# An unused tile of 224 bytes at the top of the right side of SBUF

## The chip, the cores and the metric

One Trainium2 chip, one of its cores. The metric is the time of one execution on the device in microseconds (us), the median of several runs. A single execution is also recorded by the hardware profiler, and every number about single instructions below is from that record. SBUF has 128 partitions; an address here is a number of bytes within a partition.

## The reference, cut to what matters

Attention with two mixes over the heads ("talking heads"), then two feed-forward blocks, all in float32:

```python
# q, k, v: (2, 12, 448, 64)
scores = einsum('bhij,hg->bgij', q @ k.T / 8, w_pre)
attn   = softmax(scores, axis=-1)
x      = einsum('bhij,hg->bgij', attn, w_post) @ v     # -> (896, 768)
h = x @ moe_w_in                                       # (768, 2048)
x = where(h > 0, h, exp(min(h, 0)) - 1) @ moe_w_out    # (2048, 768)
h = x @ moe2_w_in
out = (h * sigmoid(h)) @ moe2_w_out                    # (896, 768)
```

## The kernel before, in words

The order of all work is written out by hand; nothing is moved by a scheduler. The program has two parts.

**Attention** (functions `qk_pair`, `premix`, `postmix`, `av_pair`). In steps of 20 query rows TensorE computes the scores `pq` of a pair of heads (L107, K tiles `kt` stream through, Q tiles `qt` are the weights), VectorE and ScalarE write them to the tile `s`, a DMA on SP's queue (`relayout`, L137) lays them out as `blk`, and TensorE mixes the heads (`pre`, L149), then, after the softmax, mixes again (`post`, L188) and multiplies with V (`av`, L214). These matmuls are in float32 and use a quarter of the array each, four side by side.

**Two feed-forward blocks** (`moe_in`, `moe_out1`, `moe_in`, `moe_out2`). Here each product is split into high and low parts of type float32r, and three of the four part products are added up, so one chunk of weights gives three matmuls for each 128 rows of the contraction. All of these use the whole array and load new weights (128 columns) for each matmul:

- `ph` (L488): weights are the converted chunk `we`, the activations `x` stream through, 448 columns. 1152 matmuls: 576 in each block.
- `po` (L541): weights `we`, the gated activations `g` (`ge` for the first three) stream through, 448 columns. 576 matmuls.
- `py` (L561 to L563): weights `g` (`gf`), the chunk `we` streams through, 384 columns. 672 matmuls.

The weight chunks come from HBM as 64-bit numbers (`wr`), ScalarE and VectorE turn them into float32 (`wc`) and into the high and low parts (`we`) while TensorE works on earlier chunks.

**Where the tiles lie.** SBUF is shared out from both ends. Pools opened with `side="left"` grow upwards; pools with `side="right"` grow downwards from the end of the tile space, byte 229,344, which is 895 x 256 + 224. On the right lie:

- pool `qkt`: `kt` (later `x0`, the half of `x` for the first batch), `qt` (later three buffers of `we`);
- pool `s0`: `s` (later `x1`, the other half of `x`), pool `s1`: `s` and the tile `wz` of the warm-up matmuls;
- pool `wst`, which takes the place of `s1` in the last steps of attention: `wr`, `wc` and the fourth buffer of `we`.

The sizes of all of these (3584, 6144, 21,504 and 3072 bytes) are multiples of 256, so each starts 224 bytes past a multiple of 256. The parts of `x` and `we` that a matmul reads begin at multiples of 512 bytes from the start of the tile (128 columns of `we`), of 1536 (384 columns of `we`) or of 1792 (448 columns of `x`), all multiples of 256, so they too begin 224 bytes past one. On the left, `g`, `ge`, `gf`, `blk` and V begin 128 bytes past a multiple of 256, and so do the parts of `g` that `po` and `py` read; `pe` (the softmax's output), `krn` and `a` begin 64 past one.

```python
cm_w, wp = pool("qkt", bufs=1, side="right")
cm_s0, sp0 = pool("s0", bufs=1, side="right")
cm_s1, sp1 = pool("s1", bufs=1, side="right")
# moe_in, L488: stationary we, moving x
nc.tensor.matmul(ph, wt[:, kk * P:(kk + 1) * P], xq[hf, kk][:, xi], ...)
# moe_out1, L541: stationary we, moving g
nc.tensor.matmul(po, wt[:, kk * P:(kk + 1) * P], g_out1(k0 + kk, gi, hf), ...)
# moe_out2, L561: stationary g, moving we
nc.tensor.matmul(py, gh, hi[:, w_], start=(kf == 0), stop=False)
```

Of the kernel before, what the change touches and what calls it, by code (L numbers as in the profile page):

```python
# [7 lines left out]
F32 = mybir.dt.float32  # L8
# [9 lines left out]
P = 128  # L18
# [19 lines left out]
def attn_moe_moe(ctx: ExitStack, tc: tile.TileContext, q, k, v, w_pre, w_post, w1i, w1o, w2i, w2o, out):  # L38
# [4 lines left out]
    def pool(name, **kw):  # L43
        cm = tc.tile_pool(name=name, reuse_waits="tile", **kw)
        return cm, cm.__enter__()

    cm_c, cp = pool("const", bufs=1, side="left")
    cm_w, wp = pool("qkt", bufs=1, side="right")
    cm_s0, sp0 = pool("s0", bufs=1, side="right")
    cm_s1, sp1 = pool("s1", bufs=1, side="right")  # L50
# [635 lines left out]
            moe_out2(n, a, b_)  # L686
    cm_m.__exit__(None, None, None)

    for cm in (cm_pm, cm_g, cm_c, cm_ws, cm_s0, cm_w):
        cm.__exit__(None, None, None)  # L690


# [54 lines left out]
```

## Time and profile before

| | |
|---|---|
| median of 3 runs | 657.47 us (656.14 to 660.39) |
| the profiled execution | 654.97 us |
| its span, first to last instruction | 653.2 us |
| granted TensorE clock, mean | 0.997 of 2.4 GHz |
| TensorE busy | 643.3 us, 98% |
| VectorE, ScalarE, GpSimd busy | 375.3, 331.3, 55.3 us |

In the profile PE is TensorE's matmuls and PEld its weight loads, which overlap them; DVE is VectorE, ACT ScalarE, POOL GpSimd, SP SyncE, and an engine's name with a q its queue. L488 is line 488 of the kernel. The duration of one matmul is longer than the distance to the next, since matmuls follow each other in a pipeline: what sets the time is the distance from start to start, called the pitch below. A float32 matmul of the attention appears as two records. The row `post` of L488 is `ph` as well, written to a PSUM bank that the attention had.

### The profile page before, as it was taken

To read this page: it belongs to the slowest core of one execution; us is meant where nothing else is said; L and a number is where in the kernel's file an instruction comes from. 1 tells how busy PE (TensorE), PEld (TensorE's weight loads), DVE (VectorE), ACT (ScalarE), POOL (GpSimd) and SP (SyncE) were. 2 spreads that over 40 slices of the span, in tenths; PEclk is the share of its full clock that TensorE was granted. 3 is DMA by queue.
4 is the path that set the end of the run, shared out by engine and by line. 5 is a ranking of instruction groups with operands and counts; after the bars stand their busy time and mean duration, and the time that the engine had idled before them with its cause. 6 is when DMAs were issued, how large, how long until landed. Compare 5 with 4: busy or idle time off the path is not lost.

```text
span 653.2 us, 15579 instructions
## 1 busy us (share of the span) xinstructions
PE 643.3 (98%) x6444; PEld 557.6 (85%) x6444; DVE 375.3 (57%) x767; ACT 331.3 (51%) x693; POOL 55.3 (8%) x109
## 2 busy tenths in 40 slices
PE   7989999999999999999999999999999999999997
PEld 2556666677789999999999999999999999999997
DVE  3767777887637666666443345467676775307201
ACT  3656677788647767675223233455555554205101
POOL 2222222236300000000000000000000000000000
PEclk9989999999999999999999999999999999999999
DMA  5667537763304433335323444233443355317002
GB/s 177 227 185 234 174 107 206 236 214 122 125 3 135 121 108 97 103 108 151 95 83 99 129 129 146 72 98 98 120 120 98 96 149 191 96 57 224 22 1 85
DMA packets 37243, 82.36 MB, mean 126 GB/s; under 512 B 4100, under 2 KB 18228, under 8 KB 37172
## 3 DMA queue, kind: packets, MB, share of 16 engines
q1 hardware_dynamic: 36452, 80.61, 40.6%
q8 instruction: 51, 0.84, 0.5%
q10 hardware_dynamic: 720, 0.75, 0.3%
q14 instruction: 20, 0.16, 0.1%
HBM read 59.24 MB, written 2.75 MB: 95 GB/s over the span
## 4 chain that ended last, share of the span: by engine, by line
PE 98%; DMA 0%; issue 0%; ACT 0%; DVE 0%; ACTq 0%
PE ph L488 35%; PE po L541 18%; PE pre L149 8%; PE av L214 7%; PE post L188 6%; PE py L561 6%; PE py L562 6%; PE py L563 6%; PE pq L107 5%; PE post L488 1%; PE warm L250 1%; DMA blk<-s 0%; ACT L237 0%; ACT pe L163 0%; DVE nmx L155 0%
## 5 line engine op out<-in xcount | busy, mean ns | idle before, releaser
L488 PE MATMUL ph<-x,we 128*128 128x448 f32 x1116 | 228.1, 366 | 0.0
L488 PEld LDWEIGHTS ph<-x,we 128*128 128x128 f32 x1116 | 209.1, 188 | 19.4 <-issue 3.0
L541 PE MATMUL po<-g,we 128*128 128x448 f32 x468 | 99.5, 362 | 0.0
L541 PEld LDWEIGHTS po<-g,we 128*128 128x128 f32 x468 | 87.8, 188 | 5.8
L393 ACT ACTIVATE wr<-wr 128x384 f32<-128x384 f32 x132 | 70.7, 547 | 32.2 <-DMA wr<-in_w1o_dram 17.8
L436 DVE TENSOR_TENSOR we<-wc,we 128x768 fp32r<-128x768 f32 (+1 forms) x63 | 58.7, 932 | 45.2 <-ACT we L427 42.3
L163 ACT ACTIVATE pe<-pre,nmx 124x448 f32<-124x448 f32 (+1 forms) x92 | 57.4, 628 | 43.0 <-DVE nmx L155 42.5
L415 DVE SCALAR_TENSOR_TENSOR wc<-wr,wc 128x384 int32<-128x384 int32 x132 | 72.0, 545 | 5.5
L427 ACT CAST we<-wc 128x768 fp32r<-128x768 f32 (+1 forms) x63 | 50.8, 807 | 42.2 <-PE py L563 30.7
L188 PEld LDWEIGHTS post<-krn,pe 60*64 60x64 f32 x2520 | 49.8, 136 | 20.4 <-issue 15.0
L561 PE MATMUL py<-we,g 128*128 128x384 f32 x182 | 61.7, 339 | 0.0
L563 PE MATMUL py<-we,g 128*128 128x384 f32 x182 | 61.6, 339 | 0.0
L562 PE MATMUL py<-we,g 128*128 128x384 f32 x182 | 61.6, 338 | 0.0
L155 DVE TENSOR_REDUCE nmx<-pre 124x1 f32<-124x448 f32 (+1 forms) x92 | 53.1, 619 | 14.5 <-PE pre L149 13.7
L149 PE MATMUL pre<-blk,kpre 64*64 64x448 f32 (+1 forms) x360 | 53.6, 568 | 2.0 <-DMA blk<-s 1.2
L188 PE MATMUL post<-krn,pe 60*64 60x60 f32 x2520 | 50.5, 220 | 2.1 <-issue 2.1
L176 POOL TENSOR_SCALAR krn<-kps,sum 124x60 f32<-124x60 f32 (+1 forms) x92 | 40.9, 459 | 126.4 <-DVE sum L172 95.7
L107 PE MATMUL pq<-kt,qt 64*64 64x448 f32 (+2 forms) x384 | 50.2, 547 | 0.0
L413 DVE TENSOR_SCALAR wc<-wr 128x384 int32<-128x384 int32 x132 | 45.9, 348 | 0.0
L214 PE MATMUL av<-a,v 128*64 128x120 f32 (+1 forms) x768 | 45.6, 265 | 0.0
L503 ACT ACTIVATE e<-ph 128x448 f32<-128x448 f32 x32 | 17.4, 545 | 50.6 <-PE ph L488 50.6
L214 PEld LDWEIGHTS av<-a,v 128*64 128x64 f32 x768 | 36.9, 136 | 2.8 <-issue 0.3
(59 smaller groups left out, 624.8 us busy)
## 6 DMA issues: line engine op xcount, KB each, us to landing
blk<-s SPq DMA_DIRECT2D x90, 210.0 KB
wr<-in_w1i_dram SPq DMA_DIRECT2D x32, 384.0 KB
wr<-in_w2i_dram SPq DMA_DIRECT2D x32, 384.0 KB
wr<-in_w2o_dram SPq DMA_DIRECT2D x32, 384.0 KB
wr<-in_w1o_dram SPq DMA_DIRECT2D x24, 384.0 KB
v<-in_v_dram SPq DMA_DIRECT2D x16, 192.0 KB
wr<-in_w1o_dram SPq DMA_DIRECT2D x12, 256.0 KB
qt<-in_q_dram SPq DMA_DIRECT2D x8, 360.0 KB
```

Of the source, the lines that this page charges most:

```text
L107: nc.tensor.matmul(pq[e][HS * c:HS * c + n], qT[T][half, p, HS * c:HS * c + n], kT[b, p][half], start=True, stop=True, tile_position=(e * ...
L149: nc.tensor.matmul(pre[s][r][HS * c:HS * c + HS], kpre[o], blkb[o, s % NBUF, c], start=True, stop=True, tile_position=(HS * r, HS * c))
L188: nc.tensor.matmul(w[c][HS * u:HS * u + HS, r, j * BW:(j + 1) * BW], pexp[s][r][o, m * HS:(m + 1) * HS], kr[s][r][o].rearrange("p h i -> p ...
L214: nc.tensor.matmul(avt[T][e * D:(e + 1) * D, p % 3, :m], vall[b][:NV, h, j], amap[T][:NV, j * H + h, :m], start=j == 0, stop=j == 3, tile_ ...
L393: nc.scalar.activation(hf, hf, AF.Prelu, scale=2.0 ** -112, alpha=2.0 ** 32)
L415: nc.vector.scalar_tensor_tensor(cc, r[:, :, 1], 3, cc, op0=ALU.logical_shift_left, op1=ALU.bitwise_or)
L436: nc.vector.tensor_tensor(lo[:, :m], wbits[n][:, :m].bitcast(F32), hi[:, :m], op=ALU.subtract)
L488: nc.tensor.matmul(ph, wt[:, kk * P:(kk + 1) * P], xq[hf, kk][:, xi], start=(n_ == 0), stop=(n_ + 1 == len(terms)))
L541: nc.tensor.matmul(po, wt[:, kk * P:(kk + 1) * P], g_out1(k0 + kk, gi, hf), start=(k0 == 0 and n_ == 0), stop=(k0 + kn == KF and n_ == 3 * ...
L561: nc.tensor.matmul(py, gh, hi[:, w_], start=(kf == 0), stop=False)
L562: nc.tensor.matmul(py, gh, lo[:, w_], start=False, stop=False)
L563: nc.tensor.matmul(py, gl, hi[:, w_], start=False, stop=(kf == KF - 1))
```

## The change

A pool named `align` is opened on the right side ahead of all others and holds one tile of 56 float32 numbers, 224 bytes per partition, which nothing reads or writes. All right-hand pools that follow begin 224 bytes lower, at byte 229,120 = 895 x 256, so that every tile on the right starts at a multiple of 256. The tiles on the left stay where they are. Every engine and queue has the same instructions in the same order as before.

```diff
     cm_c, cp = pool("const", bufs=1, side="left")
+    cm_al, al = pool("align", bufs=1, side="right")
+    al.tile([P, 56], F32, name="align")
     cm_w, wp = pool("qkt", bufs=1, side="right")
     cm_s0, sp0 = pool("s0", bufs=1, side="right")
     cm_s1, sp1 = pool("s1", bufs=1, side="right")
@@
-    for cm in (cm_pm, cm_g, cm_c, cm_ws, cm_s0, cm_w):
+    for cm in (cm_pm, cm_g, cm_c, cm_ws, cm_s0, cm_w, cm_al):
         cm.__exit__(None, None, None)
```

## Rows read from the trace of the kernel before

**Rows 1.** The page: busy time, share of the span and instructions of each engine.

```profile
PE 643.3 (98%) x6444; PEld 557.6 (85%) x6444; DVE 375.3 (57%) x767; ACT 331.3 (51%) x693; POOL 55.3 (8%) x109
```

**Rows 2.** Chain that ended last, in time order: start, length, engine, line, instructions merged.

```profile
6.50 5.47 PE pq L107 x42
11.97 2.88 DMA blk<-s
14.99 1.40 PE pre L149 x6
...
157.85 1.42 PE ph L488 x6
...
189.44 7.50 PE post L488 x36
196.93 102.14 PE ph L488 x504
299.08 115.20 PE po L541 x576
414.28 116.74 PE ph L488 x576
```

**Rows 3.** Busy time in stretches: PE, PEld, DVE, ACT, POOL (instructions), clock, DMA share, GB/s.

```profile
531.02:653.00 121.98, 118.71 (x672) 118.39 (x671) 41.24 (x77) 29.95 (x51) 0.00 (x0) 1.00 0.32 103
```

**Rows 4.** Weight loads of the three products, by shape: busy us, mean ns, idle before.

```profile
L488 PEld LDWEIGHTS ph<-x,we 128*128 128x128 f32 x1116 | 209.1, 188 | 19.4 <-issue 3.0
L541 PEld LDWEIGHTS po<-g,we 128*128 128x128 f32 x468 | 87.8, 188 | 5.8
L561 PEld LDWEIGHTS py<-we,g 128*128 128x128 f32 x182 | 34.1, 188 | 0.0
```

**Rows 5.** Timeline at the start of attention: weight loads of `pq`, one row per pass.

```profile
7.24 0.14 PEld L107 LDWEIGHTS pq<-kt,qt 64*64 64x64 f32 x4 [0.24 <-issue]
...
7.99 0.14 PEld L107 LDWEIGHTS pq<-kt,qt 64*64 64x64 f32 x4 [0.23 <-issue]
...
11.37 0.14 PEld L107 LDWEIGHTS pq<-kt,qt 64*64 64x64 f32 x4 [0.24 <-issue]
...
11.75 0.14 PEld L107 LDWEIGHTS pq<-kt,qt 64*64 64x64 f32 x4 [0.24 <-issue]
```

**Rows 6.** Who waited for a DMA: us in total, times, longest us.

```profile
ACT wr L393 <- DMA wr<-in_w1o_dram: 17.8, 16, 1.7
...
ACT wr L393 <- DMA wr<-in_w2o_dram: 9.9, 9, 2.1
...
PE pre L149 <- DMA blk<-s: 1.2, 1, 1.2
...
PEld pre L149 <- DMA blk<-s: 1.1, 2, 0.6
```

**Rows 7.** The conversion's instructions: min/median/max ns, first and last start us.

```profile
L415 DVE SCALAR_TENSOR_TENSOR wc<-wr,wc x132: 423/559/561, 120.9 to 614.8; 128x384 int32<-128x384 int32 x120, 128x256 int32<-128x256 int32 x12
```

**Rows 8.** Line 415 in the stretch in which `wr` and `wc` lie on the left.

```profile
115.00:190.00 75.00, 3.35 (x6) 1.00 0.46 150
```

## The prediction

> **What bounds the kernel now.** I read the page's busy times first: TensorE is busy for 643.3 of 653.2 us [rows 1]. A busy TensorE can still be waiting inside its pipeline, so the chain that ended last comes next. From 196.93 us to the end it holds nothing but matmuls, in three unbroken pieces and a fourth that the stretches show [rows 2, 3]. The reader is to divide each piece by its count, since what an instruction costs here is its pitch:
>
> - `ph`, first block: 102.14 us for 504, 202.66 ns each; second block: 116.74 us for 576, 202.67 ns each.
> - `po`: 115.20 us for 576, 200.00 ns each.
> - `py`: 118.71 us for 672, 176.65 ns each.
>
> At 2.4 GHz, which the stretch grants in full (clock 1.00), 448 columns take 448 / 2.4 = 186.67 ns and 384 take 160.00. What each matmul costs beyond its columns is therefore 16.0 ns in `ph`, 13.3 in `po` and 16.7 in `py`. That is the observation on which everything rests: `ph` and `po` have the same shape, the same number type and the same source of weights (`we`, on the right), and yet `ph` is 2.67 ns slower, every time. They differ in the operand that streams: `x` lies on the right, 224 bytes past a multiple of 256 and so 32 past a multiple of 64; `g` lies on the left, 128 past a multiple of 256, which is a multiple of 64. `py` streams `we` from the right, and if it had `po`'s surplus it would take 160.00 + 13.33 = 173.33 ns, 3.32 less than it does.
>
> A weight operand at that odd start seems to cost nothing. The weight loads take 188 ns whether they read `we` from the right (`ph`, `po`) or `g` from the left (`py`) [rows 4], and of the pitches, the one with the odd start in the weights alone (`po`) is the one with the least surplus, while adding odd weights to an odd stream (`ph` against `py`) doesn't raise the surplus (16.0 against 16.7).
>
> **The change part by part.** Nothing is added to a queue or moved in one; what changes is where addresses begin. I go through who reads or writes a tile on the right.
>
> *`ph`, 1152 matmuls.* The stream `x` moves to a multiple of 256. If the odd start is what separates it from `po`, its pitch becomes 200.00 ns: 504 x 200.00 = 100.80 us in place of 102.14, 576 x 200.00 = 115.20 in place of 116.74, and for the 72 in and right after the last steps of attention (36 of them in the row of 7.50 us, the others in six rows like the one of 1.42 us) 72 x 2.67 ns = 0.19 us. Together 1.34 + 1.54 + 0.19 = 3.07 us. All of it lies on the path, since nothing waits between these matmuls.
>
> *`po`, 576 matmuls.* The stream `g` stays where it is; only the weights move. By the argument on weights: 0.
>
> *`py`, 672 matmuls.* The stream `we` moves. With `po`'s surplus it takes 672 x 173.33 = 116.48 us in place of 118.71: 2.23 us, on the path to within the last copy and store.
>
> The bounds of these terms: 0 from below, if the odd start isn't the cause. From above, the nearest row for a pitch with less surplus is `pq`, whose passes of four follow each other every 375.8 ns (7.24 to 11.75 us, 13 rows, twelve steps) [rows 5]; two times 448 columns take 373.3 ns, so 2.5 ns are left for the surplus. Were all three products to come down to 2.5 ns over their columns, `ph` would save 13.5 ns, `po` 10.8 and `py` 14.2, together 15.6 + 6.2 + 9.5 = 31.3 us. I take the value by `po`'s row, which is nearest: same shape, same type, new weights for every matmul, which `pq` has not (it is float32, each record slower, a quarter of the array).
>
> *`pq`, 384 records.* Its stream `kt` moves too. But it is at the odd start now and its surplus is 2.5 ns on a pass, so there is next to nothing to win: 48 pairs of heads with two passes each, at most 96 x 2.5 ns = 0.2 us; I take 0. `pre`, `post` and `av` read only tiles on the left: 0.
>
> *DMAs.* `kt`, `qt` and `wr` are written on the right, and `relayout` reads `s` there. TensorE waits for a DMA in two places near the start, 1.2 and 1.1 us in all, behind the 2.88 us of the first `relayout` in the chain [rows 2, 6]. The many waits on `wr` (17.8 and 9.9 us) are ScalarE's and lie beside an unbroken run of matmuls, so they cost nothing now and would give nothing. For the start the bounds are 0 and the 2.3 us that TensorE waits there; no row shows a DMA's time at two alignments, so I take 0. [...]
>
> *ScalarE, VectorE.* They write `s` and convert `wr` to `we` on the right. Line 415 took 3.35 / 6 = 0.558 us where its tiles were on the left (64 past a multiple of 256), and its median over all is 0.559 [rows 7, 8], most of them at the odd start: no sensitivity, and no place on the path behind 197 us.
>
> **Sum:** 3.07 + 2.23 = 5.30 us. From the profiled execution's 654.97 us that gives 649.7. The profiled one lies 2.5 us below the median of the runs shown, 657.47; from the median it is **652.2 us**, 0.8% less. A change within 1% either way is about what a measurement of this kernel can't tell from none.
>
> **The rivals.**
>
> 1. *Nothing changes: the start isn't the cause.* `x` and `we` differ from `g` also in lying in the upper part of SBUF (`we` from byte 161,760 up, `x` from 167,904, `g` below 140,416), and 224 bytes don't change that. For it speaks that `pq` streams from the very top at the odd start with a surplus of only 2.5 ns, so an odd start need not cost. Against it, `pq` takes its columns at half the rate, by its pass of 375.8 ns for 448 columns, and so may have room to hide a late read. Time: 657.5 us. [...]
>
> 2. *A deeper gain: either operand at the odd start costs the full surplus, and two cost no more than one.* Then `po`'s 13.3 ns would come from its weights, and `py`'s and `ph`'s from either, and all three come down to the 2.5 ns of `pq`: 31.3 us, 626.2 us. For it: the surpluses are alike (13.3 to 16.7), and each of the three products has exactly one or two operands on the right. Against it: `po` and `py` then have the same fault in different operands and differ by 3.3 ns, and the weight loads last 188 ns at either start. [...]
>
> 3. *Slower: the two operands collide when both begin in the same half of 256 bytes, modulo 128.* In `ph` both begin at 224 and it pays 2.67 ns more than `po`, whose operands begin at 224 and 128. After the change the operands of `po` and `py` begin at 0 and 128, equal modulo 128, while `ph` still has both at the same place. Then `po` takes on 2.67 ns x 576 = 1.5 us and `py`, if it adds as much to what it has, 672 x 2.67 = 1.8 us: 657.47 + 3.3 = 660.8 us. It decides itself in `po`: if its pitch leaves 200.00 upwards, this is it. Against it: `py` has the largest surplus now, with operands at 224 and 128.
>
> **How the numbers follow.** The forecast gets 0.62: one clean difference of equal products, and `py` agrees with it. Nothing 0.22, the deeper gain 0.09, the collision 0.07. The predicted time is the forecast's, 652.2. Its own range is the 5.3 us with the bounds of start and `pq` (0 to 2.5 us more) and the spread of a median of runs (they reached from 656.14 to 660.39), 649 to 654. The range for 8 in 10 must take in "nothing" as well, 657.5 and a spread of about 1 us; below, 9.3 us under the median covers the forecast with its bounds added, and leaves the deeper gain out: 648.0 to 658.5. Faster by over 1% means below 650.9: the deeper gain and, of the forecast, the part in which the start of attention or the weights give another 1.3 us, about a quarter: 0.09 + 0.16 = 0.25. Slower by over 1% needs twice the collision's price: 0.02. Within 1%: 0.73.
>
> **What would show each step.** In the chain of the changed kernel the piece of 504 `ph` should last 100.8 us, that of 576 `ph` 115.2, that of 576 `po` still 115.2, and the stretch of 672 `py` 116.5. `ph` down and `py` not would mean that the cause is in the pairing of operands; all at their old values is rival 1; `po` below 115 is rival 2, above it rival 3. The first `relayout` in the chain shows what the DMAs win. The prediction is wrong if these pitches move by other amounts, or if the attention part, for which I have put 0, changes its time.

## The result, and the profile after

The changed kernel is slower: 661.18 us median (657.75 to 667.10, 12 runs) against 656.32 (653.11 to 660.39, 12 runs), a ratio of 1.0073 with a 95% interval of 1.0046 to 1.0100. I had forecast 652.2.

The profiled execution took 658.56 us, 3.59 more than the one before. Its chain of work that ended last, in order of time (start, length, engine, line, matmuls merged), answers to [rows 2]; lines have moved by two, so `ph` is L490 and `po` L543:

```profile
11.60 2.88 DMA blk<-s
...
188.88 7.50 PE post L490 x36
196.38 102.14 PE ph L490 x504
298.52 117.50 PE po L543 x576
416.02 119.03 PE ph L490 x576
```

The stretch of `py`, which answers to [rows 3] (PE, PEld, DVE, ACT and POOL busy, clock, DMA share, GB/s):

```profile
535.05:656.80 121.75, 118.27 (x672) 117.95 (x671) 41.22 (x77) 29.80 (x51) 0.00 (x0) 1.00 0.33 103
```

The reader is to set the pieces side by side. The first `ph` block lasts 102.14 us, as before to the hundredth, although both of its operands have moved. `po`, for which I had put nothing, went from 115.20 to 117.50 us (200.00 to 203.99 ns a matmul), the second `ph` block from 116.74 to 119.03 (202.67 to 206.65 ns), with the same tiles as the first one, and `py` from 118.71 to 118.27 (176.65 to 176.00 ns). That is 2.30 + 2.29 - 0.44 = 4.15 us more. The feed-forward blocks begin 0.56 us earlier (188.88 against 189.44 us), which leaves the 3.59. The first `relayout` in the chain lasts 2.88 us in both.

### The profile page after: what moved, and what is told of

Same layout as the page of the kernel before. It is cut to its first block, busy times and chain, and to the rows that moved or that the text cites. A ratio compares the mean times of both kernels' runs of the same rounds, so it can differ in the third digit from the quotient of the medians.

```text
span 656.8 us, 15579 instructions
## 1 busy us (share of the span) xinstructions
PE 646.5 (98%) x6444; PEld 558.3 (85%) x6444; DVE 374.9 (57%) x767; ACT 331.1 (50%) x693; POOL 55.2 (8%) x109
## 4 chain that ended last, share of the span: by engine, by line
PE 98%; DMA 0%; issue 0%; ACT 0%; DVE 0%; ACTq 0%
PE ph L490 35%; PE po L543 18%; PE pre L151 8%; PE av L216 7%; PE post L190 6%; PE py L565 6%; PE py L563 6%; PE py L564 6%; PE pq L109 5%; PE post L490 1%; PE warm L252 1%; DMA blk<-s 0%; ACT L239 0%; ACT pe L165 0%; DVE nmx L157 0%
## 5 line engine op out<-in xcount | busy, mean ns | idle before, releaser
L490 PE MATMUL ph<-x,we 128*128 128x448 f32 x1116 | 230.4, 367 | 0.0
L490 PEld LDWEIGHTS ph<-x,we 128*128 128x128 f32 x1116 | 209.1, 188 | 21.8 <-issue 3.0
L543 PE MATMUL po<-g,we 128*128 128x448 f32 x468 | 101.3, 366 | 0.0
L543 PEld LDWEIGHTS po<-g,we 128*128 128x128 f32 x468 | 87.9, 188 | 7.6
L549 DVE TENSOR_TENSOR x<-po,x 128x448 fp32r<-128x448 f32 x12 | 7.5, 624 | 57.1 <-ACT x L548 57.1
```

## The experiments

Below, **distance** is the start of the operand that streams, less the start of the weights, modulo 256. By the tiles' places, before and after the change:

| | before | after |
|---|---|---|
| `ph`: `x` - `we` | 0 | 0 |
| `po`: `g` - `we` | 128 - 224 = 160 | 128 - 0 = 128 |
| `py`: `we` - `g` | 224 - 128 = 96 | 0 - 128 = 128 |

Theory A is that this distance sets the pitch. Theory B is the prediction's, that the start of the right-hand tiles does. Theory C is that each execution falls into a step of its own; theory D, that what ran just before decides.

**Both kernels once more**, unchanged.

> The kernel before, unchanged: a second recorded execution and a comparison with itself. Theory A (the distance between the starts of a matmul's two operands sets the pitch): pitches as in the first record, 202.67 ns in both ph blocks, 200.00 in po, 176.67 in py; ratio 1.000. Theory B (the start of right-hand tiles sets it): the same. Theory C (the pitch of a stage is a step that TensorE falls into anew in each execution, whatever the addresses): at least one of the four stages shows another pitch, 4 ns or so away, and the ratio still lies within 0.3% of 1.

> The changed kernel, unchanged: a second recorded execution. Theories A and B: pitches as in its first record, 202.67 ns in the first ph block, 204.00 in po, 206.67 in the second ph block, 176.00 in py; ratio to before 1.007. Theory C: other pitches than in its first record in at least one stage; ratio anywhere from 1.000 to 1.010.

The kernel before against itself gave 1.0017 (0.9985 to 1.0050), the changed one 1.0065 (1.0037 to 1.0094). The chains of the second records, of the kernel before and then of the changed one:

```profile
192.72 7.50 PE post L488 x36
200.22 102.14 PE ph L488 x504
302.37 115.20 PE po L541 x576
417.56 116.74 PE ph L488 x576
```

```profile
190.27 7.50 PE post L490 x36
197.77 102.14 PE ph L490 x504
299.91 117.50 PE po L543 x576
417.41 119.03 PE ph L490 x576
```

Each piece is the first record's to the hundredth: in two records of each of these two kernels the pitches belong to the program, and theory C falls for them. What differs between these records is the attention: the feed-forward blocks of the kernel before start at 192.72 us here and at 189.44 in [rows 2]. That start lay between 188.36 and 194.03 us in the nine records of the whole program, in no order of the pads: 5.7 us, where the runs of the kernel before lay 7.3 us apart (653.11 to 660.39).

**The distance kept, all starts moved; and the distance moved, the right side left alone.** The first has the change and 32 bytes on the left, so that `g` stands at 160 and `we` at 0; the second has no pad on the right and 224 bytes on the left, so that `g` stands at 96 and `we` at 224.

```diff
+    cm_ll, ll = pool("alignl", bufs=1, side="left")
+    ll.tile([P, 8], F32, name="alignl")       # the second: [P, 56], and no pool "align"
     cm_c, cp = pool("const", bufs=1, side="left")
+    cm_al, al = pool("align", bufs=1, side="right")
+    al.tile([P, 56], F32, name="align")
```

> The change, and 32 unused bytes on the left as well, so that the distance between tiles on the right and on the left is what it was before, modulo 256, while all starts are moved. Theory A (distance): po 200.00 ns and the second ph block 202.67, ratio 1.000. Theory B (starts on the right): as the change, po 204.00, second ph block 206.67, ratio 1.007. Theory C: pitches that fit neither; ratio 0.998 to 1.010.

> No pad on the right, 224 unused bytes on the left: starts on the right as before, the distance between right and left as after the change, modulo 256. Theory A (distance): po 204.00 ns, second ph block 206.67, ratio 1.007. Theory B (starts on the right): po 200.00, second ph block 202.67, ratio 1.000. Theory C: pitches that fit neither; ratio 0.998 to 1.010.

Ratios: 1.0003 (0.9973 to 1.0032) and 1.0065 (1.0032 to 1.0098). The chain of the first:

```profile
200.60 102.14 PE ph L492 x504
302.75 115.20 PE po L545 x576
417.95 116.74 PE ph L492 x576
```

The chain of the second:

```profile
195.86 102.14 PE ph L490 x504
298.00 117.50 PE po L543 x576
415.50 116.75 PE ph L490 x576
```

And the stretch of `py` in the second:

```profile
532.25:654.00 121.75, 118.27 (x673) 117.95 (x671) 41.22 (x77) 30.14 (x51) 0.00 (x0) 0.99 0.32 103
```

With all right-hand tiles at multiples of 256 and the old distance, every piece is as before the change (`py` too, at 118.71 us); with the right side where it was and the new distance, `po` takes 117.50 and `py` 118.27, as after the change. That is theory A for `po` and `py`, and theory B falls. One piece didn't follow: the second `ph` block took 116.75 us in the second kernel and not 119.03. Its distance is 0 in all of these, so the distance alone doesn't fix it.

The second kernel's ratio isn't accounted for by this record. Its pieces come to 2.30 + 0.01 - 0.44 = 1.87 us more, a ratio of 1.0028, just below the interval that was measured; the recorded execution, 655.84 us, was the second shortest of the twelve. In other executions the second `ph` block may have been slower, as expected; no record shows it, so theory C isn't excluded for that block.

**The distance by itself.** A kernel of nothing but series of 100 matmuls, each with a new load of weights:

```python
def series(b, wo, mo, n, count=100):           # starts in bytes, n columns
    t = bank(b)
    for i in range(count):
        w0 = wo // 4 + 128 * (i % 6)
        m0 = mo // 4 + 512 * (i % 6)
        nc.tensor.matmul(t[:, :n], wt[:, w0:w0 + 128], mv[:, m0:m0 + n], ...)
    return t
```

> None of the reference is computed (the output is zeros): series of 100 float32r matmuls with a weight load each, 448 or 384 columns, both operands in tiles that start 128 bytes past a multiple of 256. The stream's start is moved against the weights' start in steps of 32 bytes from 0 to 480, then the same with the weights 96 bytes on, then by 4, 8, 16 and 48 bytes; a pause parts the series, and at the end six follow each other without one. Theory A (distance): 448 columns take 200.0 ns at a distance of 160 bytes (stream minus weights), as po before, 204.0 at 128, as po after, and 202.67 or 206.67 at 0, as ph; 384 columns 176.67 at 96 and 176.0 at 128; moving both operands by 96 bytes changes nothing. Theory B (start of one operand): with the weights moved on by 96 bytes the row of pitches is shifted by 96 bytes or flat. Theory D (the distance sets the pitch only by what TensorE was doing before, a step kept from the stage ahead): series apart show one pitch for all distances, and the six without a pause differ.

Its chain, one row for a series: 448 columns at distances 0, 32, ... 224 (eight rows), 384 columns at 0, 96, 128, 160 and 192, and 448 columns with the weights 96 bytes on and the stream at 0, 96, 128 and 224, so at distances 160, 0, 32 and 128:

```profile
35.51 20.55 PE b L71 x100
...
56.73 20.93 PE b L71 x100
...
78.32 20.29 PE b L71 x100
...
99.28 20.81 PE b L71 x100
120.75 20.68 PE b L71 x100
...
142.10 20.30 PE b L71 x100
163.06 20.51 PE b L71 x100
...
184.23 20.73 PE b L71 x100
...
375.08 17.62 PE b L71 x100
...
429.76 17.95 PE b L71 x100
448.32 17.88 PE b L71 x100
466.81 17.94 PE b L71 x100
485.36 17.62 PE b L71 x100
...
521.84 20.29 PE b L71 x100
...
585.35 20.55 PE b L71 x100
606.56 20.29 PE b L71 x100
...
669.95 20.68 PE b L71 x100
```

A series holds a hundred pitches and some 0.29 us for its first start and its last end (20.29 us where the pitch is `po`'s 200). The pitches, worked out so:

| distance | 0 | 32 | 64 | 96 | 128 | 160 | 192 | 224 |
|---|---|---|---|---|---|---|---|---|
| 448 columns, ns | 202.6 | 206.4 | 200.0 | 205.2 | 203.9 | 200.1 | 202.2 | 204.4 |
| 384 columns, ns | 173.3 | 173.2 | 173.3 | 176.6 | 175.9 | 176.5 | 173.3 | 173.4 |

The reader is to find the kernel's pitches in it: `po` before at 160 and after at 128, `py` before at 96 and after at 128, and `ph` at 0. With both operands moved by 96 bytes the pitch goes with the distance (the last four rows), and from 256 to 480 the row repeats, each series to within 0.01 us. The exception is a distance of 32: it gave 20.93 us at first, and 20.29, so 200.0 ns, both at 288 and with the weights 96 bytes on, each time after a series at a distance of 0 and a pause. Finer steps gave 206.6 ns at 4 bytes, 206.4 at 8 and 202.3 at 16. So theory A holds, with a period of 256 bytes, and some distances have more than one pitch.

The six series without a pause bear on theory D. Read from the starts of their matmuls, a distance of 160 took 200.0 ns as the first of them and 206.7 as the last, after 384 columns at 96; a distance of 0 took 202.7 after 160 and after 128.

**What the series ahead does.** Pairs of 60 matmuls without a pause, a first series and a second.

> None of the reference is computed. 25 pairs of series without a pause between them: five first series (448 columns at a distance of 128, 160 and 64 bytes, 384 columns at 96 and 192), each followed by each of five others (448 columns at 0, 32, 64 and 160, 384 columns at 192). Theory A alone: the second series' pitch is the same after each first one: 202.67, 200.00 or 206.67, 200.00, 200.00, 173.33 ns. Theory A with a step kept from the entry: the second series at a distance of 0, 32 and 160 takes either of two pitches (202.67 or 206.67; 200.00 or 206.67; 200.00 or 206.67) according to the first one, and at 64 and 192 one alone.

Rows of its chain, second series only (L77, 60 matmuls): a distance of 0 after 448 columns at 128; a distance of 64 after 128; a distance of 160 after 128; 384 columns at 192 after 128; a distance of 0 after 160; 160 after 64; a distance of 0, of 64, of 160 and 384 columns at 192, each after 384 columns at 192.

```profile
27.09 12.17 PE b L77 x60
...
79.08 12.03 PE b L77 x60
...
104.84 12.39 PE b L77 x60
...
130.96 10.62 PE b L77 x60
...
155.02 12.18 PE b L77 x60
...
358.70 12.03 PE b L77 x60
...
526.09 12.40 PE b L77 x60
...
574.45 12.03 PE b L77 x60
...
598.32 12.40 PE b L77 x60
...
622.56 10.42 PE b L77 x60
```

60 pitches of 200.0, 202.67 and 206.67 ns are 12.00, 12.16 and 12.40 us. A distance of 160 takes 200 after 64 and 206.67 after 128; a distance of 0 takes 202.67 after 160 and 206.67 after 384 columns at 192; a distance of 64 takes 200 after each of the five. So theory D is half true: where a distance has several pitches, a series falls into one at its entry and keeps it. What chooses is not shown, and it isn't the series ahead alone: 160 after 384 columns at 96 took 12.02 us here (200 ns) and 206.7 ns in the six above. The pair in the order of the changed kernel, 0 after 128, took the low pitch (the first row), as in the six above. Each pair ran once.

I was wrong on 384 columns at 192, which took 10.42 us (173.7 ns) once, 10.49 or 10.50 (174.8 to 175.0) three times and 10.62 (177.0) once. A distance of 32 showed a third value as well, 12.28 us (204.7 ns) after each of the two series of 384 columns.

**The change, and `g` moved to 64.** 192 bytes on the left beside the change, so that `po` has a distance of 64 and `py` of 192.

```diff
+    cm_l, lp = pool("padl", bufs=1, side="left")
+    lp.tile([P, 48], F32, name="padl")
```

> The change, and 192 unused bytes on the left, so that g stands 64 bytes past the residue of we; x and we both begin at multiples of 256 as in the change. Theory A: po 200.0 ns, py 173.33, ph 202.67 in the first block and 202.67 or 206.67 in the second; against before 2.2 us less or, with the high step, 0.1 us more: ratio 0.997 to 1.000. Theory B: as the change, ratio 1.007.

Ratio 0.9981 (0.9955 to 1.0007), within the range for theory A. Its chain and its stretch of `py`:

```profile
303.67 115.21 PE po L545 x576
418.88 116.74 PE ph L492 x576
```

```profile
535.62:656.50 120.88, 117.38 (x673) 117.06 (x671) 41.24 (x77) 29.91 (x51) 0.00 (x0) 1.00 0.33 104
```

The loss of the change is gone with all right-hand tiles still at multiples of 256. The second `ph` block, entered from a `po` of 200 ns, has the low pitch. `py` takes 117.38 / 672 = 174.67 ns, above the 173.33 expected: close to the value that three of the five pairs gave at its distance of 192.

**All streams at 64.** No pad at the top; instead gaps that put `x` and `g` 64 bytes past the residue of `we`, for each of its four buffers. The lines that open and close the pools are left out here.

```diff
+    lp.tile([P, 24], F32, name="padl")         # left, ahead of "const"
     cm_w, wp = pool("qkt", bufs=1, side="right")
+    g1.tile([P, 48], F32, name="gap1")         # right, own pool
     cm_s0, sp0 = pool("s0", bufs=1, side="right")
+    g2.tile([P, 16], F32, name="gap2")         # right, own pool
     cm_s1, sp1 = pool("s1", bufs=1, side="right")
@@
     load_q(0)
+    wp.tile([P, 16], F32, name="gap0")
```

> The kernel before with unused gaps so that x begins 64 bytes past the residue of we, modulo 256, and g as well; so the stream stands at a distance of 64 in ph and po and of 192 in py, where the series by themselves took 200.00 and 173.33 ns. Theory A (the distance modulo 256 sets the pitch): both ph blocks 200.0 ns, po 200.0, py 173.33; 1152 x 2.67 + 672 x 3.33 = 5.3 us less than before, ratio 0.992. Theory B (each operand's own start): g and x begin 224 past a multiple of 256 and we 160 past one, so none is aligned: no gain, ratio 1.000 or above. Theory D (entry alone decides): ph keeps 202.67 or 206.67.

It took 651.17 us (9 runs) against 657.20 for the kernel before: ratio 0.9916 (0.9887 to 0.9946). Its chain and its stretch of `py`:

```profile
189.95 7.40 PE post L495 x36
197.35 100.80 PE ph L495 x504
298.15 115.20 PE po L548 x576
413.35 115.20 PE ph L495 x576
```

```profile
528.55:648.50 119.95, 116.49 (x673) 116.16 (x671) 41.21 (x77) 30.11 (x51) 0.00 (x0) 1.00 0.33 105
```

Both `ph` blocks take 200.00 ns and `py` 116.49 / 672 = 173.35: 1.34 + 1.54 + 2.22 and 0.1 in the row of 36, 5.2 us. None of the operands begins at a multiple of 256: `we` stands 160 past one, `x` and `g` 224. This version beats both kernels. `py` stands at a distance of 192 here as in the kernel just above, where it took 0.89 us more, so that part of its gain hangs on which pitch it fell into.

**`x` alone at 64**, `g` left at its old distance of 160 from `we` (192 bytes on the left in place of 96).

```diff
-    lp.tile([P, 24], F32, name="padl")
+    lp.tile([P, 48], F32, name="padl")
```

> As the kernel with all streams at 64, but g stands 160 bytes past the residue of we, as before the change; so only x is moved against we, to a distance of 64. Theory A: both ph blocks 200.0 ns, po 200.0, or 206.67 with the high step that a distance of 160 also showed, py 176.67 as before; with the low step 3.1 us less than before, ratio 0.995. Theory B: no gain, since x and we begin off a multiple of 256 as before, ratio 1.000.

Ratio 1.0034 (1.0006 to 1.0062): slower, with `ph` improved. Its chain:

```profile
200.95 100.80 PE ph L495 x504
301.75 119.03 PE po L548 x576
420.79 115.21 PE ph L495 x576
```

Both `ph` blocks are at 200 ns, 3.0 us less, and `po` has fallen onto the high step of its distance, 119.03 / 576 = 206.65 ns, 3.83 us more; `py` is as before, 118.70 us. In the pairs a distance of 160 entered from 64 took the low one, so the step can't be read off from the distance ahead alone.

## Why the prediction was wrong

**The step that failed** is the one in which `ph` and `po` were compared: "They differ in the operand that streams: `x` lies on the right, 224 bytes past a multiple of 256 [...] `g` lies on the left, 128 past". The difference of 2.67 ns was real, and it was in the addresses. But the two differ in the distance between their operands as well (0 against 160), and I gave it to the stream's own start. The kernel with both sides moved and the kernel with the left alone moved show that the start by itself does nothing, and that `po` and `py` go with the distance.

- *`ph`, forecast 3.07 us less: wrong.* Both operands lie on the right and moved together, so the distance stayed 0 and the first block kept 202.66 ns. The second block took on 2.29 us in both records of the changed kernel, though its operands have the same places as in the first. Its 206.65 ns is the second of the two pitches, 202.67 and 206.67 ns, that the series show at a distance of 0. Why it fell into that one stays open. After a `po` of 200 ns this block had the low pitch in all four records; but after a `po` of 203.99 ns it had the high one in the changed kernel and the low one with the left alone moved, and in the pair and the six series with the order 0 after 128 it was low too. So 2.29 of the 4.15 us are shown to be a step between two pitches of one distance, and what sets off the step is not shown.
- *`po`, forecast 0: wrong.* Moving the weights against a stream that stays changes the distance from 160 to 128: 2.30 us more. The argument that odd weights cost nothing took the two starts as two separate costs that add up. The weight loads that I read for it last 188 ns at `po`'s distance of 160 and at 128, so that row could not show it.
- *`py`, forecast 2.23 us less: wrong in cause and size.* It took 0.44 us less, and the same 0.44 with the right side where it was: the distance went from 96 to 128. Its 3.32 ns over 173.33 could be had, but by a distance of 192.
- *`pq`, `pre`, `post`, `av`, DMAs, conversion, forecast 0: not contradicted*, as far as the attention's own spread of 5.7 us lets one see. The first `relayout` lasts 2.88 us in both, so its DMA won nothing that the chain shows.

The rivals: *nothing changes* had the first `ph` block right and nothing else. *The deeper gain* fell: no series of float32r came below 200.0 and 173.3 ns, so the surplus of 13.3 ns is there at the best distance tried. The columns' own share of the pitch, 186.67 ns for 448 by the prediction, stood in no row of before; the series bear it out, since these two best pitches lie 26.7 ns apart for 64 columns, 0.417 ns a column at a granted clock of 1.00, and 448 columns at that are 186.7. *The collision* was right that the distance counts and that `po` would show it, and its 660.8 us is near the 661.18 measured, but not by its own terms: `po` paid 2.30 and not 1.5, `py` gained 0.44 where it was to lose 1.8, and its rule (equal modulo 128) fits neither the table nor the second `ph` block. Its argument against itself, that `py` had the largest surplus at unequal starts, speaks against any rule in which equal starts are the costly ones.

The size of my forecast, 5.3 us, turned out to be what a distance of 64 for the streams of `ph` and `po` gives (5.2 us in the record, 0.9916 of the kernel before), by a change to other addresses than the one made. That the two sizes agree is no credit to the reasoning by starts: the best values of the series happen to be the surplus of `po`, which stood on a good step before the change.

Up to 6.67 ns of a pitch of 200 hang on where one operand lies relative to the other and, at some distances, on the step. What in TensorE or SBUF does this no run shows, and why 64 is good (200.0 ns), 96 bad (205.2) and some distances have several pitches stays open.

## What to carry to other kernels

Before aligning anything, compare matmuls of one shape by pitch and write down the places of both operands, not of one. Where float32r matmuls load new weights each time, the distance of stream and weights modulo 256 is worth a table from a kernel of nothing but series; then choose a distance whose pitch doesn't depend on what ran before; at 448 columns that was 64, which gave 200.0 ns in every series, pair and kernel here. A pad that moves one pool moves every operand in it against all others: list each pair that it changes.

## What the hardware showed that I had not expected

- A matmul of 448 float32r columns takes from 200.0 to 206.7 ns, one of 384 from 173.3 to 177.0, by the distance of its operands modulo 256 and, at some distances, by a step that it falls into at the entry.
- A stage keeps the pitch that it falls into for hundreds of matmuls: 576 at 206.65 ns in `po` at a distance of 160 in one program, 576 at 200.00 at the same distance in another.
